# Shifting the pairs of chunks in the last batch of an attention and feed-forward kernel by one

## The chip, the cores and the metric

The kernel runs on one core of one Trainium2 chip. The metric is device time in microseconds (us); lower is better. A core has five engines that each run their own instructions in order: TensorE (PE; its weight loads are a row of their own, PEld), VectorE (DVE), ScalarE (ACT), GpSimd (POOL) and SyncE (SP). DMA transfers are issued from the queues of SP, ACT and POOL.

## The reference

```python
def _attn_ref(q, k, v, tau):                      # each (4, 5824, 256), f32
    qn = q / (norm(q, axis=1) + 1e-06)
    kn = k / (norm(k, axis=1) + 1e-06)
    s = kn.transpose(0, 2, 1) @ qn / tau          # (4, 256, 256)
    a = softmax(s, -1)
    return v @ a

def _moe_ref(x, w1, w2, w3, w_out):               # x = the attention's output, (23296, 256)
    return (((x @ w1) * (x @ w2)) @ w3) @ w_out   # w1, w2: (256, 1024), w3: (1024, 1024), w_out: (1024, 256)
```

For each of four batches, the small matrix of scores is folded into w1 and w2 (`Wf`), and w3 and w_out are multiplied into one matrix W (`W_sb`, 1024 x 256). What remains for a batch is: a = v Wf1, b = v Wf2, and the output (a * b) W.

## The kernel before, in words

**Chunks and blocks.** The 5824 tokens of a batch are cut into 12 chunks: 0 to 10 of 512 tokens and chunk 11 of 192. The 1024 columns of `Wf` are 8 blocks of 128. A *normal* block of a chunk (`normal`) is two matmuls for a and two for b, each of 512 columns; ACT casts a to bf16 (L988), DVE multiplies it with b out of PSUM (L1020), and the result is a part of `abh`, the chunk's a * b.

**Blocks by seven.** In the last batch (3) some blocks of two neighbouring chunks, c and c+1, are made together by a scheme of Strassen's kind: seven matmuls of 512 columns (X, T, X, Y, X, Z, X in `by_seven`) in place of eight, for three ACT copies (Y, t, as) and four DVE operations (Z, bs, and two products into `abh`, L1054 to L1085). It needs sums of the weights (`wsum`, made by DVE when the weights are folded) and sums of the tokens (`tsum`, four POOL operations of 512 columns for a pair, L682 to L688). `BY_SEVEN` says for each pair how many of its 8 blocks are made that way; the other blocks of the pair are normal. `plan` writes the order of the normal blocks (`todo`), and for each block by seven the place in that order from which it may start, moved by `W_SHIFT`; `TOKENS_AHEAD` says how many places before it the token sums are queued.

**Outputs.** When all 8 blocks of a chunk are done, `queue_out` appends its output to the list `outs`, which leaves in order of `out_key`: only its first line may go on. The output is made in one of three ways. *Plain products* (chunks in `PLAIN`): 32 matmuls of 256 columns, in two halves of four steps (`emit_half`, L1101), one PSUM bank each. *Seven products* (all others): a second scheme of that kind, seven products of 8 matmuls of 128 columns (prodA, prodB, prodC, L830). It needs four sums of parts of `abh`, in order, each of 1024 columns: POOL makes them (L790, L792), or, for chunks in `BY_DMA`, transfers do: two plain ones from SP's queue that copy two parts (L808, L809), and four from POOL's queue that add into memory (L800). *Singles*: chunk 11, and in the last batch chunk 10 as well, are put out one block at a time as each is done (`single`, `emit_out`, L1141), into banks that stay taken; chunk 10 uses the banks G and out2, which the scores leave free in the last batch. The outputs of the last `LAG_END` blocks of chunk 11 are held back to the very end (`ends`).

**What sets the order.** The instructions of all engines are written out by a planner in the Python of the kernel. `now` holds its reckoning of each engine's time by fixed costs (`work_on`), `free` the time at which each bank is free. `step` picks, for PE's next few matmuls, what can start first: the normal line, up to two blocks by seven, or the first line of `outs`, which is hurried or held by a credit that keeps about `HALF_BACK` steps in store. POOL's work waits in `pool_line`; `pool_due` takes the allowed one that is due first, by the number of steps until it is needed times `STEP`, or for token sums by `SLOT` and `T_EARLY`. `B1_BIAS` weighs two ways for one operation of a block by seven: DVE alone (`bs`, L1073), or ACT and POOL (L1070). An agenda starts the loads of v (POOL's queue), each behind a `gate` on POOL, and, if chunk 0 is paired, its token sums at `TSUM` within the batch before.

In the kernel before, the last batch is made as pairs (0,1), (2,3), (4,5), (6,7), (8,9) with 3, 5, 5, 5 and 4 blocks by seven, and chunk 10 alone.

Of the kernel before, what the change touches and what calls it, by code (L numbers as in the profile page):

```python
# [11 lines left out]
F32 = DT.float32  # L12
BF16 = DT.bfloat16

P = 128
PIECE = 8
LAG_END = 2
BIG_BUFS = 31
HALF_BACK = 12
LANDING = 4.0  # L20
W_SHIFT = 1
STEP = 1.9
SLOT = 1.8
T_EARLY = 0.0
N_BIAS = 0
O_BIAS = 0.05
B1_BIAS = -0.5
MM_COL = 1.0 / 2400.0
MM_FIX = 0.0025

# [2 lines left out]
def kernel(  # L33
# [14 lines left out]
    B, N, C = q.shape  # L48
    T, D = out.shape
# [15 lines left out]
    NCH = NT // 4 + 1  # L65
# [80 lines left out]
    turned_v, turned_at = {}, {}  # L146
# [404 lines left out]
        )  # L551


    BY_SEVEN = {(3, 0): 3, (3, 2): 5, (3, 4): 5, (3, 6): 5, (3, 8): 4}
    PAIRED = {b: tuple(c for b2, c in sorted(BY_SEVEN) if b2 == b) for b in range(B)}
    PLAIN = {0: (0, ), 1: (), 2: (), 3: (0, 2, 9, )}
    BY_DMA = {3: (4, 6, )}
    TSUM, WSUM0, TSUM0 = 100, 12.0, 26.0
    wsums = {}
    tsums = {}  # L560
# [95 lines left out]
    def queue_token_sums(b, c):  # L656

        until = now["PE"] + TOKENS_AHEAD * SLOT

        def step(i):  # L660
            def fn(at_):
                token_sum(b, c, i)
                if i == 3:
                    tready[b, c] = at_
            return fn

        for i in range(4):
            pool_add(
                lambda i=i: until - now["PE"] + 1.1 * (i - 3) - T_EARLY,
                (0.0, lambda: turned_at.get((b, c // 2), FAR) <= now["PE"], 1.06, step(i)),  # L670
            )

    tready = {}
# [81 lines left out]
    def out_bank(tag, ready=0.0):  # L755
        return max(free.get(tag, 0.0), ready)
# [133 lines left out]
    def plain_products(b, c, ab2, whole):  # L890

        for i in range(FT):
            yield lambda i=i: max(out_bank(f"out{i // 4}", whole), w_made[0])
            emit_half(b, c, i, ab2)

    def out_tags(b, c):
        return ("G", "out2") if (b, c) == (B - 1, NCH - 2) else ("out0", "out1")

    def single(b, c, j, ab, ready):

        yield lambda: max(
            ready, w_made[0], *(out_bank(t) for t in out_tags(b, c)), 0.0 if queued.get(b, 0) == NCH - 1 - b // (B - 1) else FAR
        )
        emit_out(b, c, j, ab)

# [40 lines left out]
    def finish(b, c, j, ready):  # L946

        key = b, c
        done_of.setdefault(key, []).append(ready)
        credit[0] = min(4.0, credit[0] + (1.0 if steps_left[0] > HALF_BACK else 0.8))  # L950
        if c == NCH - 1 or (b == B - 1 and c == NCH - 2):
            return
        if len(done_of[key]) == FT:
            queue_out(b, c, max(done_of[key]))
# [36 lines left out]
    def normal(b, c, j):  # L991

        n = chunk_cols(c)
        share_ = n / 512

        def both(w, t):
            for ct in range(CT):
                nc.tensor.matmul(  # L998
                    t[:, :n], lhsT=Wf[b][:, ct, w, j * P : (j + 1) * P], rhs=rhs_of(b, c, ct),
                    start=(ct == 0), stop=(ct == CT - 1),  # L1000
                )
            return work_on("PE", 2 * (n * MM_COL + MM_FIX))

        yield lambda: max(bank_at(), wready.get(b, 0.0))
        tag, t = take(f"a_{b}_{c}_{j}", cols=n)
        r = both(0, t)
        a_sb = cast(t, f"as_{b}_{c}_{j}", n)
        cast_at = free[tag] = work_on("ACT", 0.07 + 0.395 * share_, r)
        yield lambda: bank_at()
        tag, t = take(f"b_{b}_{c}_{j}", cols=n)  # L1010
        r = both(1, t)
        if c == NCH - 1:
            if b % 2 == 0 and j == 0:
                lefts[b // 2] = work.tile([P, FT, 2, P + LEFT], BF16, tag="left", name=f"left_{b}", bufs=1)
            two = lefts[b // 2][:, j, b % 2, :]
            nc.vector.tensor_mul(two, a_sb[:, :n], t[:, :n])
            ab = two[:, :P] if b % 2 == 0 else two[:, LEFT:]
        else:
            ab = place(b, c, j)
            nc.vector.tensor_mul(ab, two_halves(a_sb), two_halves(t))  # L1020
        ready = free[tag] = work_on("DVE", 0.065 + 0.533 * share_, r, cast_at)
        last_ab[:] = [ab, ready]
        finish(b, c, j, ready)
        if c == NCH - 1 and b == B - 1 and j >= FT - LAG_END:
            ends.append(lambda only=None: emit_out(b, c, j, ab, only))
        elif c == NCH - 1 or (b == B - 1 and c == NCH - 2):
            put_out(b, c, single(b, c, j, ab, ready), 1)

    ends = []
# [61 lines left out]
    def emit_half(b, c, i, ab2):  # L1091

        h, jj = divmod(i, 4)
        if i % 4 == 0:
            out_tiles[b, c, h] = psum.tile([P, 2, D], F32, tag=f"out{h}", name=f"o_{b}_{c}_{h}", bufs=1)
        if i == 0:
            out_tiles[b, c] = work.tile([P, 4, D], F32, tag="o_sb", name=f"osb_{b}_{c}", bufs=3)
        t, o = out_tiles[b, c, h], out_tiles[b, c]
        for j in (2 * jj, 2 * jj + 1):
            for k in range(2):  # L1100
                nc.tensor.matmul(  # L1101
                    t[:, k, :], lhsT=ab2[j // 4][:, h, j % 4, k * P : (k + 1) * P], rhs=W_sb[:, j, :],
                    start=(j == 0 and k == 0), stop=(j == FT - 1), skip_group_check=True,
                )
        work_on("PE", 4 * (D * MM_COL + MM_FIX))
        read = now["PE"] + LATE["PE"]
        if i == 3:
            nc.scalar.copy(o[:, 0:2, :], t)
            free["out0"] = work_on("ACT", 0.475, read)
        elif i == FT - 1:  # L1110
            if b == B - 1:
                nc.scalar.copy(o[:, 2:4, :], t)
                free["out1"] = work_on("ACT", 0.475, read)
            else:
                nc.vector.tensor_copy(o[:, 2:4, :], t)
                free["out1"] = work_on("DVE", 0.6, read)
            rows = out[b * N : b * N + NT * P, :].rearrange("(p i) c -> p i c", i=NT)
            nc.sync.dma_start(out=rows[:, 4 * c : 4 * c + 4, :], in_=o)

    def emit_out(b, c, j, ab, only=None):  # L1120
# [6 lines left out]
        else:  # L1127
            lhs = [ab[:, i // 2, i % 2 * P : (i % 2 + 1) * P] for i in range(4)]
        if j == 0:
            if b == B - 1 and not small:  # L1130
                held.update(("G", "out2"))
            out_tiles[b, c] = [
                psum.tile([P, 2, D], F32, tag=tag, name=f"o_{b}_{c}_{tag}", bufs=1)
                for tag in out_tags(b, c)[: len(lhs) if small else 2]
            ]
# [278 lines left out]
                c += 1  # L1414
        return todo, sevens

    TOKENS_AHEAD = 2
    token_at = {}
    stuck = [0]
    credit = [0.0]  # L1420
# [2 lines left out]
    def step(b, todo, sevens, at_n):  # L1423

        run_due()
        scores_due(progress[0])
        while later:
            later.pop(0)()
        pool_due()
        if lines["N"] is None and todo:  # L1430
            if (b, at_n[0]) in token_at and (b > 0 or at_n[0] > 0):
                queue_token_sums(b, token_at.pop((b, at_n[0])))
            lines["N"] = Line(normal(b, *todo.pop(0)))
            at_n[0] += 1
        while sevens and sevens[0][0] < at_n[0] and len(lines["W"]) < 2:
            lines["W"].append(Line(by_seven(b, *sevens.pop(0)[1:])))
        choices = [(max(now["PE"], w.est()), i, w) for i, w in enumerate(lines["W"])]
        if lines["N"] is not None:
            choices.append((max(now["PE"], lines["N"].est()) + N_BIAS, 3, lines["N"]))
        if outs:  # L1440
            hurry = credit[0] > 0.0 or steps_left[0] > 2 * HALF_BACK or not todo
            choices.append((max(now["PE"], outs[0].est()) + (-0.02 if hurry else O_BIAS), 4, outs[0]))
        if not choices:
            return
        when, kind, line = min(choices, key=lambda x: x[:2])
        if when > FAR / 2:
            now["PE"] += 0.2
            stuck[0] += 1
            assert stuck[0] < 1000, (b, at_n, choices, pool_line, held, progress, steps_left)
            pool_due()  # L1450
            return
        stuck[0] = 0
        more = line.go()
        if kind == 4:
            steps_left[0] -= 1
            line.left -= 1
            credit[0] = max(credit[0] - 1.0, -1.0)
            if not more:
                outs.pop(0)
        else:  # L1460
            progress[0] += 0.5 if kind == 3 else 2 / 7
            if not more:
                if kind == 3:
                    lines["N"] = None
                else:
                    lines["W"].remove(line)
# [55 lines left out]
```

## Time and profile before

| | us |
|---|---|
| median of 3 runs | 550.21 (550.02 to 550.28) |
| the profiled execution's own time | 550.1 |
| its span, from the first to the last instruction | 548.1 |
| busy: PE, PEld | 536.1, 350.5 |
| busy: DVE, ACT, POOL | 426.5, 397.4, 416.0 |
| POOL: adds of 128x1024 (L790 and L792), one | 2.13 |
| POOL: token sums of 128x512, one | 1.15 |
| DVE: product of 128x512 (L1020), one | 0.685 |
| ACT: cast of 128x512 (L988), one | 0.563 |

The rows of the profile name a line of the kernel, the engine, the operation, output<-inputs by the program's names, the shapes and the count. A matmul's duration in the rows is longer than the distance from one to the next, since matmuls are pipelined and their ends are modelled; the distances between starts say what PE really does. The last batch's matmuls start at about 428 us; the last matmul of all starts at 543.51.

### The profile page before, as it was taken

The page shows a single profiled execution, that of the slowest core. Times are in us where ns is not written, and L with a number is a line of the kernel's source. Part 1 is how long each engine was busy: PE and PEld are TensorE (multiplying, and loading weights), DVE is VectorE, ACT ScalarE, POOL GpSimd, SP SyncE. Part 2 cuts the span into 40 slices and gives each one's busy share as a digit, 9 for nine tenths or more (in the row PEclk, how much of TensorE's full clock was granted, in tenths as well). Part 3 has the DMA queues.
Part 4 walks back from the last instruction along what each step waited for, and adds up shares of the span by engine and source line. Part 5 has one row for each costly group of instructions (what it writes and reads, how often), then busy time and mean ns, then how long its engine had stood idle before and what let it go on. Part 6 is the DMA issues. An engine that isn't in the chain of part 4 may idle for free.

```text
span 548.1 us, 12254 instructions
## 1 busy us (share of the span) xinstructions
PE 536.1 (98%) x4599; PEld 350.5 (64%) x4607; DVE 426.5 (78%) x750; ACT 397.4 (73%) x826; POOL 416.0 (76%) x343
## 2 busy tenths in 40 slices
PE   7799999999999999999999999999999999999996
PEld 4564566666677666666658666666666656566676
DVE  5477748999876888888766788888878688999962
ACT  5446648889777788888676888888777677777762
POOL 4270794979999499998996498979999946978560
PEclk9999999999999999999999999999999999999999
DMA  9999987994876848875582867776651335656513
GB/s 213 212 205 208 215 162 156 225 189 101 130 165 145 190 87 186 171 160 125 118 170 90 163 137 148 150 147 125 155 117 72 85 87 115 156 110 174 142 53 136
DMA packets 76747, 80.75 MB, mean 147 GB/s; under 512 B 54416, under 2 KB 59024, under 8 KB 76688
## 3 DMA queue, kind: packets, MB, share of 16 engines
q0 software_dynamic: 16816, 41.03, 42.7%
q1 hardware_dynamic: 59504, 38.22, 25.1%
q8 instruction: 36, 0.59, 0.4%
q10 hardware_dynamic: 368, 0.72, 0.4%
q14 instruction: 23, 0.19, 0.1%
HBM read 78.91 MB, written 23.86 MB: 187 GB/s over the span
## 4 chain that ended last, share of the span: by engine, by line
PE 92%; DMA 5%; issue 1%; ACT 1%; DVE 1%; POOL 0%; DVEq 0%; POOLq 0%
PE a L998 25%; PE b L998 25%; PE prodA L830 13%; PE prodC L830 6%; PE G L216 6%; PE X L983 3%; PE prodB L830 3%; DMA k<-in_k_dram 3%; PE o L1101 3%; PE fold L449 2%; DMA q<-in_q_dram 2%; PE w L1290 1%; PE o_out L1141 1%; PE Y L983 1%; PE Z L983 1%; PE T L983 1%
## 5 line engine op out<-in xcount | busy, mean ns | idle before, releaser
L1020 DVE TENSOR_TENSOR abh<-as,b 128x512 bf16<-128x512 bf16 x308 | 210.3, 685 | 66.8 <-ACT as L988 44.3
L988 ACT CAST as<-a 128x512 bf16<-128x512 f32 (+1 forms) x340 | 191.0, 563 | 68.3 <-PE a L998 55.6
L998 PE MATMUL a<-vT,Wf 128*128 128x512 bf16 x616 | 183.2, 379 | 0.2
L998 PE MATMUL b<-vT,Wf 128*128 128x512 bf16 x616 | 183.2, 379 | 0.0
L998 PEld LDWEIGHTS <-Wf 128*128 128x128 bf16 x1360 | 122.2, 98 | 76.9 <-issue 0.7
L790 POOL TENSOR_TENSOR S<-abh,abh 128x1024 bf16<-128x1024 bf16 x37 | 78.9, 2132 | 51.1 <-DVE abh L1020 34.5
L830 PEld LDWEIGHTS <-S 128*128 128x128 bf16 x1216 | 80.1, 98 | 23.1
L230 DVE TENSOR_TENSOR acc<-acc,sq 128x512 f32<-128x512 f32 x132 | 91.6, 694 | 1.2 <-ACT sq L213 0.3
L792 POOL TENSOR_TENSOR S<-S,abh 128x1024 bf16<-128x1024 bf16 x37 | 78.8, 2128 | 2.7
L792 POOL TENSOR_TENSOR S<-abh,S 128x1024 bf16<-128x1024 bf16 x37 | 79.4, 2147 | 0.1
L792 POOL TENSOR_TENSOR S<-abh 128x1024 bf16<-128x1024 bf16 x37 | 78.9, 2132 | 0.1
L830 PEld LDWEIGHTS <-abh 128*128 128x128 bf16 x968 | 64.1, 98 | 20.4 <-issue 0.5
L843 ACT COPY osb<-prodA 128x256 f32<-128x256 f32 x113 | 42.2, 373 | 16.5 <-PE prodA L830 16.0
L216 PE MATMUL G<-k,q 128*128 128x256 bf16 x276 | 52.4, 273 | 0.0
L216 PEld LDWEIGHTS <-q 128*128 128x128 bf16 x276 | 27.0, 98 | 32.1
L830 PE MATMUL prodA<-comb_T,S 128*128 128x128 bf16 x608 | 46.3, 219 | 0.0
L213 ACT ACTIVATE sq<-q 128x512 f32<-128x512 bf16 x69 | 43.9, 636 | 0.0
L213 ACT ACTIVATE sq<-k 128x512 f32<-128x512 bf16 x69 | 43.4, 629 | 0.0
L850 DVE TENSOR_TENSOR osb<-osb,prodC 128x256 f32<-128x256 f32 x76 | 31.5, 414 | 4.4 <-ACT osb L843 3.5
L130 POOL DMA_DIRECT2D q<-in_q_dram x27 | 15.2, 563 | 11.7 <-DMA q<-in_q_dram 5.6
L830 PE MATMUL prodB<-W_sb,abh 128*128 128x128 bf16 x312 | 23.8, 219 | 0.0
L830 PE MATMUL prodA<-W_sb,abh 128*128 128x128 bf16 x312 | 23.8, 219 | 0.0
(175 smaller groups left out, 649.2 us busy)
## 6 DMA issues: line engine op xcount, KB each, us to landing
out_dram<-osb SPq DMA_DIRECT2D x44, 512.0 KB, 3.4
k<-in_k_dram POOLq DMA_DIRECT2D x19, 512.0 KB, 8.2
v<-in_v_dram POOLq DMA_DIRECT2D x19, 512.0 KB, 6.7
q<-in_q_dram POOLq DMA_DIRECT2D x18, 512.0 KB, 5.3
w<-in_moe_w_dram POOLq DMA_DIRECT2D x4, 512.0 KB, 16.7
k<-in_k_dram POOLq DMA_DIRECT2D x4, 320.0 KB, 7.3
v<-in_v_dram POOLq DMA_DIRECT2D x4, 320.0 KB, 4.3
S<-abh SPq DMA_DIRECT2D x4, 256.0 KB, 3.0
```

What stands on the lines that cost most here:

```text
L213: nc.scalar.activation(out=sqs[0][:, :, part, :], in_=src[:, o : o + 2, :], func=AF.Square)
L216: nc.tensor.matmul(G[:, ct, :], lhsT=qt[:, i, ct * P : (ct + 1) * P], rhs=kt[:, i, :], start=(pr == 0 and part == 0 and ct == 0), stop=(pr ...
L230: nc.vector.tensor_add(accs[n], accs[n], sqs[0][:, part - 2])
L790: nc.gpsimd.tensor_add(x, a21, a22)
L792: nc.gpsimd.tensor_sub(x, *{2: (sums[1], a11), 3: (a11, a21)}.get(i) or (a12, sums[2]))
L830: nc.tensor.matmul(st[nm][:, i, :], lhsT=a[:, j, i * P : (i + 1) * P], rhs=w[j], start=(first and j == 0 and i == 0), stop=(j == 3), skip_ ...
L843: nc.scalar.copy(quarter(r, d), st[nm])
L850: nc.vector.tensor_add(quarter(r, d), quarter(r, d), st[nm])
L983: nc.tensor.matmul(dst, lhsT=lhsT, rhs=rhs, start=start, stop=True, skip_group_check=True)
L988: nc.scalar.copy(a_sb[:, :n], t[:, :n])
L998: nc.tensor.matmul(t[:, :n], lhsT=Wf[b][:, ct, w, j * P : (j + 1) * P], rhs=rhs_of(b, c, ct), start=(ct == 0), stop=(ct == CT - 1),)
L1020: nc.vector.tensor_mul(ab, two_halves(a_sb), two_halves(t))
```

## The change

In the last batch, the pairs become (1,2), (3,4), (5,6), (7,8), (9,10) with 3, 5, 5, 4 and 5 blocks by seven, and chunk 0 is made alone, of normal blocks. Plain products make the outputs of chunks 1, 3, 9 and 10; chunk 10 no longer goes out block by block but by plain products in the banks G and out2, queued when all its blocks are done. The sums of chunk 5 are made by transfers, in place of those of chunks 4 and 6. Seven settings of the planner change with it.

```diff
-LAG_END = 2
+LAG_END = 4
-W_SHIFT = 1
-STEP = 1.9
-SLOT = 1.8
-T_EARLY = 0.0
+W_SHIFT = -1
+STEP = 1.6
+SLOT = 2.2
+T_EARLY = 1.0
-B1_BIAS = -0.5
+B1_BIAS = -1.0
...
-    BY_SEVEN = {(3, 0): 3, (3, 2): 5, (3, 4): 5, (3, 6): 5, (3, 8): 4}
+    BY_SEVEN = {(3, 1): 3, (3, 3): 5, (3, 5): 5, (3, 7): 4, (3, 9): 5}
-    PLAIN = {0: (0, ), 1: (), 2: (), 3: (0, 2, 9, )}
-    BY_DMA = {3: (4, 6, )}
+    PLAIN = {0: (0, ), 1: (), 2: (), 3: (1, 3, 9, 10, )}
+    BY_DMA = {3: (5, )}
...  # queue_token_sums: the piece of the pair's second chunk must be turned
-                (0.0, lambda: turned_at.get((b, c // 2), FAR) <= now["PE"], 1.06, step(i)),
+                (0.0, lambda: turned_at.get((b, (c + 1) // 2), FAR) <= now["PE"], 1.06, step(i)),
...  # plain_products
-            yield lambda i=i: max(out_bank(f"out{i // 4}", whole), w_made[0])
+            yield lambda i=i: max(out_bank(out_tags(b, c)[i // 4], whole), w_made[0])
...  # single
-            ready, w_made[0], *(out_bank(t) for t in out_tags(b, c)), 0.0 if queued.get(b, 0) == NCH - 1 - b // (B - 1) else FAR
+            ready, w_made[0], *(out_bank(t) for t in out_tags(b, c)), 0.0 if queued.get(b, 0) == NCH - 1 else FAR
...  # finish
-        if c == NCH - 1 or (b == B - 1 and c == NCH - 2):
+        if c == NCH - 1:
             return
...  # normal
-        elif c == NCH - 1 or (b == B - 1 and c == NCH - 2):
+        elif c == NCH - 1:
             put_out(b, c, single(b, c, j, ab, ready), 1)
...  # emit_half
         if i % 4 == 0:
-            out_tiles[b, c, h] = psum.tile([P, 2, D], F32, tag=f"out{h}", name=f"o_{b}_{c}_{h}", bufs=1)
+            if (b, c) == (B - 1, NCH - 2):
+                held.update(("G", "out2"))
+            out_tiles[b, c, h] = psum.tile([P, 2, D], F32, tag=out_tags(b, c)[h], name=f"o_{b}_{c}_{h}", bufs=1)
...  # emit_out
-            if b == B - 1 and not small:
-                held.update(("G", "out2"))
...
-    TOKENS_AHEAD = 2
+    TOKENS_AHEAD = 1
```

## The prediction

> **What bounds the kernel now.** I read the page first, then the busy time by stage, then the order of TensorE's own instructions, and last the rows of the engines that feed it. From the page:
>
> ```profile
> span 548.1 us, 12254 instructions
> PE 536.1 (98%) x4599; PEld 350.5 (64%) x4607; DVE 426.5 (78%) x750; ACT 397.4 (73%) x826; POOL 416.0 (76%) x343
> PE 92%; DMA 5%; issue 1%; ACT 1%; DVE 1%; POOL 0%; DVEq 0%; POOLq 0%
> ```
>
> and all long waits of PE (us in total, times, longest):
>
> ```profile
> PE sqq L277 <- DMA q<-in_q_dram: 4.8, 4, 1.7
> PE warm_I-94_95 L248 <- DVE ones_pp L94: 1.4, 1, 1.4
> ```
>
> PE is busy nearly always, the chain that ended last is PE for 92%, and the two waits lie at the start of the program. But a busy PE is only an occupied one, so I looked at starts. In the windows of the last batch (columns: stretch, length, then busy us and count of PE, PEld, DVE, ACT, POOL, clock, DMA share, GB/s):
>
> ```profile
> 428.00:440.00 12.00, 11.95 (x99) 7.24 (x98) 9.15 (x16) 8.46 (x18) 9.50 (x9) 1.00 0.39 91
> 440.00:450.00 10.00, 9.91 (x54) 5.07 (x52) 8.41 (x14) 7.38 (x15) 3.53 (x2) 1.00 0.43 116
> 490.00:510.00 20.00, 20.00 (x181) 12.62 (x180) 18.58 (x33) 15.14 (x33) 17.72 (x15) 1.00 0.62 167
> 521.90:531.50 9.60, 9.60 (x94) 6.30 (x92) 5.99 (x11) 5.97 (x12) 8.41 (x4) 1.00 0.14 56
> ```
>
> The clock is 1.00 throughout. DVE is next to full from 450 to 521 (18.58 of 20) and half empty after; POOL is half empty at the start. The timeline of PE (start, us, count) gives what one matmul really takes:
>
> ```profile
> 445.90 0.38 PE L983 MATMUL T<-tsum,wsum 128*128 128x512 bf16 x1
> 446.36 0.59 PE L998 MATMUL a<-vT,Wf 128*128 128x512 bf16 x2
> 446.79 0.38 PE L983 MATMUL X<-tsum,wsum 128*128 128x512 bf16 x1
> 541.87 1.91 PE L1141 MATMUL o_out<-W_sb,left 128*128 128x256 bf16 x16
> ```
>
> Two matmuls of 512 columns and the next: 446.79 - 446.36 = 0.43, so 0.216 each. Sixteen of 256 columns: (1.91 - 0.27) / 15 = 0.109. The same reading gives 0.0825 for 192 columns and 0.0557 for 128. With those pitches I went through all starts from 428 to the last at 543.51: only four gaps over 0.03 us are more than the pitch, 0.25 at 446.36 (446.36 - 445.90 - 0.216), 0.05 at 457.46, 0.08 at 479.11, 0.05 at 518.47. A fifth, 0.216 at 429.39, is exactly one matmul: the groups count 21 T for 22 blocks by seven, so a record is missing and nothing stood still. **So the last batch holds 0.43 us of standing PE in 115.8 us; the rest is work at full pace.** The Trainium skill ("Perfetto Trace Analysis", section "Identifying the Most-Contended Engine") warns off matmul occupancy and has headroom read from LDWEIGHTS busy, here 64%. By that rule a third of the batch would be open, an estimate of 0.36 x 115.8 = 42 us; the starts above leave 0.43, and the measurement decides.
>
> The one larger gap, in the chain in order of time:
>
> ```profile
> 444.24 0.68 DVE abh L1020
> 444.92 0.61 DVE bs L1073
> 445.62 0.70 DVE abh L1078
> 446.36 0.59 PE a L998 x2
> ```
>
> Three DVE operations in a row, and PE waits for the bank that the last one frees.
>
> **The change part by part.** *PE's work.* Blocks by seven: 3+5+5+5+4 = 22 before, 3+5+5+4+5 = 22 after, 7 matmuls of 512 each in place of 8. Chunks by plain products: 0, 2, 9 and, one block at a time, 10 before; 1, 3, 9, 10 after: four each, 32 matmuls of 256 each. Chunks by seven products: seven each, 56 matmuls of 128 each. Chunk 11 and its 16 outputs stay. PE's sum does not move by one matmul, so the change can only move the 0.43 us, and what follows the last matmul.
>
> *Sums by transfers.* One chunk in place of two: four adds on POOL come, four issues of adding transfers go, and two plain 256 KB transfers of SP's queue.
>
> ```profile
> L792 POOL TENSOR_TENSOR S<-abh 128x1024 bf16<-128x1024 bf16 x5 | 10.7, 2133 | 0.0
> L790 POOL TENSOR_TENSOR S<-abh,abh 128x1024 bf16<-128x1024 bf16 x5 | 10.6, 2126 | 16.4 <-DVE abh L1078 13.2 <-DVE abh L1085 3.2
> L682 POOL TENSOR_TENSOR tsum<-vT 128x512 bf16<-128x512 bf16 x4 | 5.0, 1242 | 0.0
> ```
>
> Four adds are 4 x 2.13 = 8.5 us; the eight issues of adding transfers at L800 took 1028, 887, 884 and 858 ns by kind, 0.91 in the mean, so four give 3.65 back. The token sums of the first pair (four of 1.15, 4.6 us) move from the end of batch 2 into batch 3. POOL in the batch: 75.3 + 8.5 + 4.6 - 3.65 = 84.8 of 115.8. It has the room: its adds sat 16.4 us waiting for blocks. Queued behind the new additions on POOL are the gates and loads of v. Before, the loads of 433.4, 451.1 and 468.1 were used by token sums at 455.9, 474.9 and 496.4, 22 us or more later; the shifted pairs need them half a pair sooner (some 10 us), so 2 to 8 us of delay on POOL cost nothing. SP loses 512 KB of transfers and its stores wait for less.
>
> *Does a POOL add slow DVE?* DVE's product L1020 took 684 ns from 438.7 to 446.3, with POOL empty, and 686 from 484.1 to 491, with it full. No cost. The Trainium skill ("Trainium Architecture — The Big Picture", section "What this means for kernel authors") says that DVE and GpSimd share a port pair under an exclusive lock; taken bluntly it would add 8.5 us to a nearly full DVE. The rows above show no such lock for these forms.
>
> *The start.* Chunk 0 runs as eight normal blocks (one DVE operation per block, not four per pair of blocks by seven), so the row of three DVE operations behind the 0.25 us gap moves off the place where the batch starts. It can come back in the next pair: I bound the batch's gaps between 0 and 1.0 (twice the four of before and a bit) and take 0.3: the three small ones (0.18) and half of the 0.25.
>
> *The end.* Now the last pair (9, 10) has five blocks by seven. From the time T at which pair (7, 8) is done, PE still has: 5x7x0.216 + 6x4x0.216 = 12.7; chunk 11, 32 x 0.0825 = 2.6; chunks 7 and 8, 112 x 0.0557 = 6.2; chunks 9 and 10, 64 x 0.109 = 7.0; chunk 11's outputs 1.75; and what is left of earlier chunks, 1.3 by the three products left at 521.9 in this trace (bounds 0 and 3.1). Sum 31.6, so T = 543.8 - 31.6 = 512.2 (510.4 to 513.5). Outputs leave in order, so chunks 9, 10 and 11 (8.7) stand behind chunk 8's last product (0.45): POOL's last sum must be there by 543.8 - 9.2 = 534.6. It starts chunk 7's and 8's eight adds at T: 512.2 + 17.0 = 529.2; before, it ended at 531.46 and its product began at 532.46. If all the last token sums fall behind T, 533.8. Cover 5.4 or 0.8 us. DVE after T: 20 operations by seven at 0.688, 6 normal at 0.684, 4 to 6 joins at 0.417: 20 us, at the 93% of the full stretch 21.5, so 533.7; the 8.7 us of outputs behind it set the limit at 535.1. Cover 1.4 us. Both just fit, and in time: I put the cost at nothing.
>
> *After the last matmul.* The copies, the two stores of ACT's queue and the closing take 548.1 - 543.8 = 4.3 us and are the same. LAG_END 4 only holds back four blocks' outputs in place of two. Chunk 10's store was issued at 542.50 and lands 3.0 later; now ACT copies both halves, and if its products end at 543.8 - 1.75 = 542.0, a copy of 0.59 makes that 542.9 and 545.9, still 1.0 us ahead of the last small store (issued at 544.66, 2.3 to land). Nothing, while that 1.0 holds.
>
> *The other settings.* STEP scales the due times of all four-add sequences alike, so the batches before keep their order; B1_BIAS chooses a path through POOL (L1070) that this trace doesn't hold once, and -1.0 chooses it less. Nothing.
>
> Sum: span 548.1 - 0.43 + 0.30 = 548.0; the profiled execution was 550.1, so 2.0 lie around the span, and the median 550.21 is 0.1 over it: **550.1 us**. What a measurement of this kernel can tell from no change is about 0.2%, 1.1 us.
>
> **The rivals.** *POOL ends last (slower).* If the last token sums and the transfers' four issues both fall behind T, POOL's last sum is at 512.2 + 17.0 + 4.6 + 3.65 = 537.5, 2.9 past 534.6, and PE stands by as much: up to 553.1, likeliest 552.1 with half the issues and some work saved for it. It decides from the point at which chunk 8's last sum ends after 534.6. For it: chunks 7 and 8 are now both on POOL, back to back. Against: 16.4 us of idle POOL before such sums.
>
> *DVE ends last (same or slower).* If the last pair starts late or DVE stays below 93%, its last product comes up to 1.3 after 535.1: 550.4 to 551.5.
>
> *All gaps go (faster, but not by what counts).* 550.21 - 0.43 = 549.8. To pass 549.1, another 0.7 would have to come out of the 4.3 us after PE, which the change doesn't touch.
>
> **How the numbers follow.** The forecast (549.8 to 550.6) 0.55; DVE last 0.15, half of it over the bound; POOL last 0.23, all over it; all gaps gone 0.05; 0.02 for what I don't see. Faster than 549.1: 0.03. Slower than 551.3: 0.23 + 0.07 + 0.01 = 0.31. Same: 0.66. The range, 549.6 to 552.4, takes in the floor with 0.2 of scatter and the larger part of POOL's case; some 0.15 lie above.
>
> **What would show it.** Right: PE busy from 428 on as before, gaps of at most 0.5 us, POOL's last 128x1024 add over before 534.6, and the same 4.3 us after the last matmul. Wrong: a gap of 1 us or more on PE between 530 and 543 ahead of a prodC released by POOL (the POOL rival) or of an L1101 matmul released by DVE (the DVE rival); or a last store that is chunk 10's.

## The result and the profile after

The changed kernel takes 551.48 us (median of 10 runs, 551.34 to 552.00) against 550.25 (550.02 to 550.51) for the kernel before in the same comparison: ratio 1.0024, 95% interval 1.0015 to 1.0032. It is 1.2 us slower, just past the 0.2% that the prediction set as its bound. The page after:

```profile
span 549.4 us, 12254 instructions
PE 537.2 (98%) x4596; PEld 350.3 (64%) x4607; DVE 425.7 (77%) x749; ACT 398.5 (73%) x827; POOL 420.7 (77%) x343
PE 89%; DMA 6%; POOL 2%; ACT 1%; issue 1%; DVE 1%; POOLq 0%; ACTq 0%; DVEq 0%
```

PE is still busy 98%, but the chain that ended last now runs through DMA for 6% in place of 5%, and through POOL for 2% in place of 0%. Where that happens stands in the windows of the last batch (stretch, length, then busy us and count of PE, PEld, DVE, ACT, POOL, clock, DMA share, GB/s):

```profile
428.00:440.00 12.00, 12.00 (x100) 7.25 (x99) 6.75 (x12) 8.16 (x17) 9.54 (x9) 1.00 0.46 105
440.00:450.00 10.00, 10.00 (x75) 5.72 (x73) 9.07 (x15) 7.53 (x16) 7.42 (x5) 1.00 0.35 101
500.00:510.00 10.00, 9.81 (x89) 6.00 (x89) 8.59 (x16) 6.53 (x16) 9.92 (x9) 1.00 0.50 104
510.00:520.00 10.00, 9.38 (x91) 5.81 (x88) 8.16 (x14) 6.69 (x16) 8.30 (x6) 1.00 0.38 108
520.00:530.00 10.00, 9.95 (x92) 6.35 (x92) 9.57 (x17) 8.02 (x17) 9.92 (x6) 1.00 0.13 54
```

The start of the batch is better than before (DVE 6.75 busy of the first 12 us in place of 9.15, PE busy throughout to 450); most of PE's idle time lies between 500 and 520. By the distances between starts, as in the prediction, PE stands 0.08 us at 441.06, 0.15 at 458.38, 0.03 at 477.98, 0.09 at 502.27, 0.30 at 503.22, 0.78 at 511.44 and 0.15 at 515.10: 1.58 us in all, against 0.43 before. (Gaps of exactly one matmul are left out here too: the page counts 4596 matmuls for 4607 weight loads.) The difference of 1.15, and 1.22 between the starts of the last matmuls (544.73 and 543.51), is the loss. The two largest gaps, in PE's timeline (503.22 - 502.70 and 511.44 - 510.23, less one and two matmuls of 0.216), and then the waits of weight loads and matmuls from 428 on (total, times, longest):

```profile
502.70 0.38 PE L983 MATMUL X<-tsum,wsum 128*128 128x512 bf16 x1
503.22 0.62 PE L830 MATMUL prodA<-comb_T,S 128*128 128x128 bf16 x8
```

```profile
509.78 0.61 PE L830 MATMUL prodA<-comb_N,S 128*128 128x128 bf16 x8
510.23 0.59 PE L998 MATMUL b<-vT,Wf 128*128 128x512 bf16 x2
511.44 0.62 PE L830 MATMUL prodC<-comb_N,abh 128*128 128x128 bf16 x8 [0.62 <-DMA abh<-abh]
```

```profile
PEld L983 <- DVE Z L1054: 1.3, 4, 0.5
PEld L830 <- POOL S L792: 1.2, 3, 0.6
PEld L830 <- DMA abh<-abh: 1.1, 1, 1.1
PE prodC L830 <- DMA abh<-abh: 0.6, 1, 0.6
```

prodC<-comb_N,abh is chunk 5's first C product. It reads S1 = a21 + a22, which the adding transfer abh<-abh makes in place. (A weight load's wait need not stop PE as long: this one waited 1.1 us, and PE stood 0.78; the gap in the starts is what counts.) The chain in order of time and POOL's timeline lead to the cause:

```profile
500.72 4.52 POOL S L792 x2
505.24 0.06 POOL S L800
505.30 0.17 issue
505.46 5.93 DMA abh<-abh
511.40 0.05 issue
```

```profile
500.09 0.92 POOL L800 DMA_DIRECT2D S<-abh  x1
500.72 2.44 POOL L792 TENSOR_TENSOR S<-abh 128x1024 bf16<-128x1024 bf16 x1
502.80 2.43 POOL L792 TENSOR_TENSOR S<-abh,S 128x1024 bf16<-128x1024 bf16 x1
504.87 1.23 POOL L800 DMA_DIRECT2D S<-S  x1
505.46 1.55 POOL L800 DMA_DIRECT2D abh<-abh  x1
506.02 2.17 POOL L682 TENSOR_TENSOR tsum<-vT,vT 128x512 bf16<-128x512 bf16 x1
```

The transfer was issued 0.59 after another and landed 5.93 later. The planner reckons 4.0 (`LANDING`), and PE's order is fixed when the program is written, so the product stands first, whatever else PE could do. Before, the two transfers of this kind landed after 3.35 and 4.29 and their products came 1.8 and 3.5 after the landing. For the first of them, in the kernel before: POOL's timeline, the landings of all its adding transfers (L800), and the product in PE's timeline (495.84 + 3.35 = 499.19, and the product at 500.95):

```profile
494.19 0.90 POOL L800 DMA_DIRECT2D S<-S  x1 [0.69 <-DMA S<-abh]
495.84 0.88 POOL L800 DMA_DIRECT2D abh<-abh  x1 [0.76 <-DVE bs L1073]
496.40 1.50 POOL L682 TENSOR_TENSOR tsum<-vT 128x512 bf16<-128x512 bf16 x1
```

```profile
DMA to landing us min/median/max: 3.2/3.3/4.3
```

```profile
500.95 0.44 PE L830 MATMUL prodC<-comb_N,abh 128*128 128x128 bf16 x5
```

In the changed kernel, the issue at 500.09 sits between two of chunk 6's adds, the second and the third: the third ends at 503.16, and PE's product that reads it starts at 503.22, after 0.30 of standing.

### The profile page after: what moved, and what is told of

Same layout as the page of the kernel before. It is cut to its first block, busy times and chain, and to the rows that moved or that the text cites. A ratio compares the mean times of both kernels' runs of the same rounds, so it can differ in the third digit from the quotient of the medians.

```text
span 549.4 us, 12254 instructions
## 1 busy us (share of the span) xinstructions
PE 537.2 (98%) x4596; PEld 350.3 (64%) x4607; DVE 425.7 (77%) x749; ACT 398.5 (73%) x827; POOL 420.7 (77%) x343
## 4 chain that ended last, share of the span: by engine, by line
PE 89%; DMA 6%; POOL 2%; ACT 1%; issue 1%; DVE 1%; POOLq 0%; ACTq 0%; DVEq 0%
PE a L998 24%; PE b L998 24%; PE prodA L830 12%; PE prodC L830 6%; PE G L216 5%; PE o L1103 3%; PE prodB L830 3%; PE X L983 3%; DMA k<-in_k_dram 3%; PE fold L449 2%; DMA q<-in_q_dram 2%; PE w L1290 1%; POOL S L792 1%; DMA abh<-abh 1%; PE o_out L1141 1%; PE Z L983 1%
## 5 line engine op out<-in xcount | busy, mean ns | idle before, releaser
L790 POOL TENSOR_TENSOR S<-abh,abh 128x1024 bf16<-128x1024 bf16 x38 | 80.9, 2130 | 51.1 <-DVE abh L1020 49.2
L792 POOL TENSOR_TENSOR S<-S,abh 128x1024 bf16<-128x1024 bf16 x38 | 80.8, 2127 | 2.8
L792 POOL TENSOR_TENSOR S<-abh,S 128x1024 bf16<-128x1024 bf16 x38 | 81.2, 2138 | 0.1
L792 POOL TENSOR_TENSOR S<-abh 128x1024 bf16<-128x1024 bf16 x38 | 81.2, 2137 | 0.1
L830 PEld LDWEIGHTS <-abh 128*128 128x128 bf16 x952 | 62.8, 98 | 20.9 <-DMA abh<-abh 1.1
```

What stands on the lines that cost most here:

```text
L790: nc.gpsimd.tensor_add(x, a21, a22)
L792: nc.gpsimd.tensor_sub(x, *{2: (sums[1], a11), 3: (a11, a21)}.get(i) or (a12, sums[2]))
L830: nc.tensor.matmul(st[nm][:, i, :], lhsT=a[:, j, i * P : (i + 1) * P], rhs=w[j], start=(first and j == 0 and i == 0), stop=(j == 3), skip_ ...
```

## The experiments

Four theories. **L** (late landing): the loss is the waits for chunk 5's adding transfers, and what their issues cost on POOL. **P**: POOL has too much to add between 500 and 530, with chunks 6, 7 and 8 on it. **N**: the shift itself puts the blocks by seven where nothing covers their chains. **S**: the seven settings cost many small gaps. Each kernel was timed beside the kernel before on the same chip; ratios are to that. "Standing" is the sum of PE's gaps from 428 on, made as above from one profiled execution of each kernel; it is good to about 0.1 us.

**One wait taken away.** Chunk 5's first C product reads another part of abh.

```diff
-        r2 = product("C", sums[1], t1, True)
+        r2 = product("C", a22 if by_dma else sums[1], t1, True)
```

> The changed kernel, with chunk 5's product C reading a part of abh in place of the sum S1 that the transfer abh<-abh makes: the transfer is still issued and lands, but PE has nothing to wait for (the output of chunk 5 leaves that sum out). Every engine's order is the same. Theory L (late landing: PE stood 0.78 us at 511.44 because the transfer issued at 505.46 took 5.93 us to land): the gap ahead of prodC<-comb_N,abh goes, all other gaps stay, 551.48 - 0.78 = 550.7 (550.5 to 550.9). Theory P (POOL is short of room in that stretch, and PE would wait at the next sum anyway): the 0.78 comes back within 10 us at another product, 551.3 to 551.6. Theory S (the new settings cost many small gaps all over the batch): 551.3 to 551.6, too.

Measured 1.0031 (1.0019 to 1.0042), standing 2.38. The 0.78 went, and 1.59 came at chunk 5's second C product:

```profile
516.78 0.62 PE L830 MATMUL prodC<-W_sb,abh 128*128 128x128 bf16 x8 [1.42 <-DMA abh<-S]
```

L's 550.5 to 550.9 was missed. P had said that the time would come back within 10 us at another product, and it did, 5.3 us further on, and longer than P gave (551.93 against 551.3 to 551.6). But what PE waits for is the next transfer, not an add of POOL. It was issued at 511.40, and landed 5.34 later, where the changed kernel's took 3.41. So I took both waits away.

```diff
-        r3 = product("C", sums[4], w22)
+        r3 = product("C", a22 if by_dma else sums[4], w22)
```

> The changed kernel, with both C products of chunk 5 reading a part of abh in place of the sums S1 and S4: all four adding transfers are still issued, in the same order, but PE waits for neither (chunk 5's output leaves these sums out). Taking S1's wait away alone let PE stand 1.59 us at S4 instead. Theory L: now nothing comes back, the gap of 0.78 is gone and the others stay: ratio to before 1.0010 (1.0004 to 1.0016), PE standing about 0.8 us in the batch. Theory P or N (something else is short there, and PE would stand at another place): 1.0020 or more.

Measured 1.0012 (1.0003 to 1.0021), standing 0.78: the gap is gone and nothing comes back. The transfers still land late here (5.92 and 4.77), and nobody waits.

**The transfers taken away.**

```diff
-                nc.gpsimd.dma_start(out=dst, in_=src, accum_op=ALU.add)
```

> The changed kernel without the four adding transfers of chunk 5 (its output leaves these additions out); the planner still reckons with them, so all other instructions keep their order. Besides the waits, their issues on POOL are gone (0.92 to 1.55 us each), which stood ahead of chunk 6's last two adds. Theory L: the 0.78 and the 0.30 at chunk 6's third sum go, PE stands about 0.5 us: ratio 1.0004 (0.9998 to 1.0010), and the adds take 2.13 us, not 2.44. Theory N: 1.0015 or more.

Measured 0.9999 (0.9990 to 1.0008), standing 0.47, as good as the 0.43 before the change. The 0.30 at 503 went as well; POOL's timeline there, and the weight loads' wait for POOL, 0.3 in place of 1.2:

```profile
499.97 2.12 POOL L792 TENSOR_TENSOR S<-abh 128x1024 bf16<-128x1024 bf16 x1
502.05 2.13 POOL L792 TENSOR_TENSOR S<-abh,S 128x1024 bf16<-128x1024 bf16 x1
```

```profile
PEld L829 <- POOL S L792: 0.3, 1, 0.3
```

Without the issue ahead of it, the third add starts 2.09 after the second in place of 2.71, so 0.62 earlier, and takes 2.12, not 2.44. The shift, the new settings, and POOL's adds for chunks 6, 7 and 8 are all still in this kernel, in which nobody makes chunk 5's sums, and together they cost nothing beyond the 0.4 us that the interval leaves open: N and S fall as causes of the loss, and L holds. POOL keeps a share that no kernel here takes apart. In the chain of the changed kernel chunk 6's adds stand right ahead of the issue at 505.46, so they made the transfer late as well; those adds without the transfers cost nothing, but the transfers without those adds were not tried.

**A second chunk by transfers.** `BY_DMA = {3: (5, 7, )}`

> The changed kernel with two chunks' sums by transfers again, 5 and 7 (the kernel before had 4 and 6): POOL has one chunk's adds for each pair, as before, and 8.5 - 3.65 = 4.9 us less to do between 500 and 530, where it was 93 to 99% busy in the changed kernel. Theory P (POOL is the engine that is short in 500 to 530, and PE's stands are the outputs' first line waiting for it): PE stands about 0.5 us in the batch, ratio to before 1.000 to 1.001. Theory L (each chunk by transfers costs a wait, as these land after 4.4 to 5.9 us and not 4.0): two such waits, ratio 1.003 to 1.005. Theory N (the shift puts the blocks by seven where nothing covers their chains, whoever makes the sums): 1.0015 to 1.003.

Measured 1.0051 (1.0039 to 1.0064), standing 3.30. The gaps to 515 are those of the changed kernel to 0.02, and chunk 7 adds its own: 1.18 at its first C product, with a landing of 6.4 us, and 0.34 at a POOL add. P wanted a gain; L's 1.003 to 1.005 was right but for 0.0001.

```profile
531.90 0.62 PE L830 MATMUL prodC<-comb_N,abh 128*128 128x128 bf16 x8 [1.01 <-DMA abh<-abh]
```

**POOL relieved by chunk 7.** `PLAIN = {..., 3: (1, 3, 7, 9, 10, )}`

> The changed kernel with chunk 7's output by plain products: no sums for it, 8.5 us less on POOL between 500 and 530, and 32 matmuls of 256 in place of 56 of 128 on PE, 3.49 - 3.12 = 0.37 us more work. Theory P: the gaps of 1.65 us in the batch fall to 0.6 or less, ratio 1.000 to 1.0015. Theory L: chunk 5's transfers stay, with their gap of 0.5 to 1.5, and 0.37 comes on top: ratio 1.003. Theory N: 1.0025 to 1.0035.

Measured 1.0027 (1.0016 to 1.0037), standing 1.62, and 0.37 more work. POOL falls from 9.92 to 4.21 of 10 in the stretch from 520, and the gaps at 503 and 511 are as they were (0.30 and 0.78), so that P falls for chunk 7's adds; N's 1.0025 to 1.0035 holds the time too, and it is the kernel without the transfers that speaks against N:

```profile
520.00:530.00 10.00, 10.00 (x69) 5.97 (x68) 8.90 (x15) 7.96 (x17) 4.21 (x3) 1.00 0.13 52
```

**No transfers at all, POOL does the sums.** `BY_DMA = {3: ()}`

> The changed kernel with no chunk's sums by transfers: chunk 5's four adds go to POOL as well (8.5 us more there, four issues of 0.9 to 1.55 us fewer). Theory L: both gaps that hang on the transfers go (0.78, and the 0.30 behind the add that an issue lengthened from 2.13 to 2.44), 550.3 to 550.7. Theory P: POOL's adds for chunks 5 to 8 in a row end later than PE needs them, 552 to 554. Theory S: 551.3 to 551.6.

Measured 1.0015 (1.0007 to 1.0024), standing 1.81 in the profiled execution, which was a shorter one (550.8). The median is 550.97: L's 550.3 to 550.7 was too low, P's 552 to 554 too high by more. The two gaps are gone, but POOL is at 9.84 of 10 from 500 and 9.92 after, and gaps of 0.07 to 0.35 come in nine places from 497 on. Only part of them is POOL's: three weight loads waited 0.9 us in all for its adds; most of the gaps stand at blocks by seven and normal blocks, and what caused those was not taken further. So chunk 5's sums don't come free on POOL either, but there they cost no more than by transfers (1.0015 against 1.0024, with intervals that overlap).

**The planner told the truth about landings.** First `LANDING = 6.0`, which also moves the issues on POOL:

> The changed kernel with LANDING 6.0 in place of 4.0: the planner reckons that a transfer of sums lands 6 us after its issue, and puts chunk 5's waiting products later in PE's order, and the issue of abh<-abh behind one token sum. Theory L: PE has other work ahead of prodC_5, its gap falls from 0.78 to under 0.2, 550.6 to 550.9; the 0.30 gap of 503.22 (a POOL add lengthened by an issue beside it) may stay. Theory P: as long as before or longer, 551.3 to 552. Theory S: 551.3 to 551.6.

Measured 1.0021 (1.0012 to 1.0030), standing 1.39: the gap at chunk 5's first C product is gone, but issues fell elsewhere between chunk 6's adds, whose last one then kept PE for 0.39, and gaps of 0.35 and 0.19 came behind. L's size was missed; by the time alone this kernel lies nearer to what P and S gave. Then only the landing, with the issues' due times left alone:

```diff
-                made[i] = at_ + LANDING
+                made[i] = at_ + 5.5
```

> The changed kernel with the planner reckoning 5.5 us in place of 4.0 from an adding transfer's issue to its landing, and the due times of the issues left alone: POOL's order stays the same, PE's differs in some ten places, with chunk 5's waiting products later. Theory L: the 0.78 gap falls under 0.2, the 0.30 stays: ratio 1.0010 (1.0005 to 1.0016). Theory N: PE has nothing else to do there and stands as long: 1.0020 to 1.0028.

Measured 1.0017 (1.0008 to 1.0026), standing 1.20. The 0.78 is gone, the 0.32 of 503 stays, and 0.25, 0.14 and 0.13 come at blocks by seven between 511 and 516. Both forecasts were missed, L's by a little. Of 0.78 half is recovered: what PE has in place of the product isn't all ready either, and that is the part of N that this kernel shows.

**Why the transfer lands late.** Chunk 6's output store of 512 KB is held back until chunk 5's.

```diff
+            if (b, c) == (3, 6):
+                held_stores.append(store)
+                return
```

> The changed kernel with chunk 6's 512 KB store of the output (issued at 507.14, beside the transfer abh<-abh that lands late) held back until chunk 5's. If the store beside it is what made that transfer slow, abh<-abh lands 4.0 to 4.4 us after its issue in place of 5.93, and the 0.78 gap goes; if the transfer queued just ahead of it or POOL's token sums behind it are, it still takes 5.5 to 6. The time says less: if PE runs ahead by 0.78, the fetch of 16 KB of instructions that fell on the transfer of S4 without S1's wait (5.34 us to land) falls on it again, and PE stands there up to 1.6 us: ratio 1.001 to 1.0035.

Measured 1.0026 (1.0016 to 1.0035), standing 1.85. From the issue (L800) to the landing: the transfer abh<-abh and then all four, first in the changed kernel, then in this one:

```profile
abh<-abh POOLq DMA_DIRECT2D x1, 256.0 KB, 5.9
DMA to landing us min/median/max: 3.3/3.5/5.9
```

```profile
abh<-abh POOLq DMA_DIRECT2D x1, 256.0 KB, 4.6
DMA to landing us min/median/max: 3.3/4.2/4.8
```

abh<-abh took 4.61 in place of 5.93 and PE's gap there is gone; 1.04 came at the second C product, whose transfer took 4.80. So 1.3 us of the lateness are the store's. The rest over the 3.3 of a transfer alone, another 1.3, goes with the transfer S<-S issued 0.59 ahead. No kernel moved that issue alone, but the traces at hand agree: in the kernel before, the second abh<-abh, 0.58 behind S<-S, with no store and no token sum beside it, took 4.29, and the first, 1.65 behind S<-S and with a token sum right behind it, took 3.35. So a token sum behind it does not make it late. The DMA queues from 505 to 512, in the changed kernel, show the two side by side:

```profile
q0 software_dynamic: 288, 0.52, 42.9%
q1 hardware_dynamic: 144, 0.52, 19.6%
```

In the packets of this trace, POOL's queue moved 48 in half a microsecond alone, and 21 to 27 beside 21 to 27 of the store. The Trainium skill ("DMA: Bandwidth & Descriptors", section "Queues, rings and completion order") says that an engine takes turns between its queues packet by packet. The equal counts fit that; the turns themselves are not seen, as the records don't name the engine.

**The parts apart.** The old pairs with one chunk by transfers, `BY_DMA = {3: (6, )}`:

> The kernel before with its old pairs and settings, but one chunk's sums by transfers in place of two (6; chunk 4's go to POOL, which then has the adds of both 4 and 5 and the token sums of a pair, 17.0 + 4.6 = 21.6 us in about 20). Theory P: PE comes to stand 0.5 to 2 us behind these adds, ratio 1.001 to 1.004. Theory L: one chunk less with a late landing, ratio 0.999 to 1.0005. Theory N: as before, 0.999 to 1.0005.

Measured 1.0035 (1.0021 to 1.0048), standing 2.33. Here P holds: with chunks 4 and 5 both on it POOL is at 9.84 and 9.92 of 10 from 490 to 510, and PE's longest gap, 0.70, is its:

```profile
505.28 0.62 PE L830 MATMUL prodC<-W_sb,S 128*128 128x128 bf16 x8 [0.54 <-POOL S L792]
```

The old pairs with the new settings:

> The kernel before with its old pairs and two chunks by transfers, and the seven new settings. Theories P, L and N all put the loss elsewhere, but the settings were chosen for other pairs: blocks by seven two places earlier and token sums one place ahead. Theory S (the settings alone cost it): 1.002 or more. The others: 0.9995 to 1.0015.

Measured 1.0045 (1.0033 to 1.0058), standing 2.52. All expected too little but S. Its gaps, up to 0.57, lie in some fourteen places from 444 to 520.

The new pairs with the old settings:

> The shifted pairs with the seven settings of the kernel before (LAG_END 2, W_SHIFT 1, STEP 1.9, SLOT 1.8, T_EARLY 0.0, B1_BIAS -0.5, TOKENS_AHEAD 2). Chunk 5's sums are still by transfers, and the two issues S<-S and abh<-abh again follow each other on POOL with token sums behind them. Theory S: the loss goes with the settings, 550.0 to 550.6. Theory L: the second of the two issues again takes over 5 us to land, and PE's gap there is 0 to 1.5 us by where the planner puts the product, 551 to 552.5.

Measured 1.0049 (1.0036 to 1.0063), standing 3.37; its transfer abh<-abh landed after 4.52, its gaps are 0.1 to 0.4 each in some fifteen places, most between 517 and 538, and none is at that product. S is wrong of the changed kernel and L says too little: pairs and settings go together, each with the other's costs 2.5 to 2.8 us, together 1.2.

Over all kernels the time follows PE's standing to about 0.5 us: 0.43 before, 0.47 at ratio 0.9999, 0.78 at 1.0012, 1.58 at 1.0024, 2.38 at 1.0031, 3.30 at 1.0051. Furthest off is the kernel in which POOL makes all the sums, with 1.81 at 1.0015.

## Why the prediction was right or wrong

**Right.** PE's work did not change; the whole loss is standing PE in the last batch. The 0.25 us gap went (0.26 in three small ones to 478 in its place). DVE did not end last: after 515.10 PE has no gap, and the last pair's five blocks by seven are covered. POOL's last add ended at 531.0, later than the 529.2 reckoned but ahead of the 534.6 given, and the 8.5 us of chunk 7's adds cost nothing (the kernel with chunk 7 plain). From the start of the last matmul to the end come 4.7 us, against 4.6 before, and the last store wasn't chunk 10's: that one landed 2.0 us ahead of the last, not 1.0 (the 3.0 from issue to landing was the median of four stores; its own took 2.6 before and after). 551.48 lies in the range of 549.6 to 552.4, and the slower side had 0.31. That is luck: the range went so far for POOL's sake, and the 0.31 was for POOL or DVE ending last, neither of which happened.

**Wrong.** 550.1 was the likeliest case, within 0.2% of no change, and it was 0.24% slower. The step that failed is "Sums by transfers": it priced chunk 5's transfers by what they do to POOL's total (3.65 us given back for the four issues that go; the four that stayed took 4.56) and never asked when they land, nor how far ahead of its product each landed in the trace of before. Those rows were there: 3.35 and 4.29 from issue to landing, 1.8 and 3.5 us to spare. In the changed kernel the transfers lost their cover twice: chunk 6's adds come first on POOL, so that the first adding transfer, whose two inputs had landed by 496.1, is issued at 500.09; and the second and third then go out together, beside a store. The bound for the batch's gaps (0 to 1.0, value 0.3) came from the four gaps of before and held no term for them; they measured 0.78 and 0.30, of a standing of 1.58 in all.

**The rivals.** POOL was the right engine in the wrong place: not chunk 8's last sum at the end, but chunk 6's third, behind an issue, and for 0.30 and not 2 us. No rival named a transfer that lands late, though the change says that it moves them.

## What to carry to other kernels

Here the order was written ahead, and PE, busy 98%, lost its time where the reckoning was wrong: most of all for a transfer, reckoned at 4.0 us and landed after 5.93. Before moving work onto or among them, list each one's issue, its landing and the start of its reader, and treat the spare time between as the thing being changed. Taking one wait away can show the next, so take them away one by one and then all. Where POOL issues a transfer between its own operations, count the operation behind it as late by a part of the issue (0.62 of 0.92 us here) and as longer (2.44 for 2.13).

## What the runs showed of the hardware

A transfer of 256 KB that adds within on-chip memory, issued from POOL, landed 3.3 us after its issue alone, 4.3 to 4.75 when issued 0.6 behind another (the kernel before, the one with the store held back, the old pairs with the new settings), and 5.9 with a 512 KB store beside it as well. A POOL add of 128x1024 took 2.40 to 2.44 us beside an issue, 2.13 otherwise.

The second C product's transfer landed after 3.41 in the changed kernel and after 5.34, 4.77 and 4.80 in three kernels with nearly the same order. In those a fetch of 16 KB of instructions (the queue marked "instruction") ran during its data, from 514.04, 513.91 and 513.11 for 0.95 to 1.45 us; in the changed kernel it came at 514.71, when the data had passed. In the first of the three (no wait for S1) all of the transfer's packets of data were done by 514.35 but eight of 2 KB, and the first of these began at 514.98, as the fetch ended. That they share one of the 16 DMA engines is inferred from this; the records don't name the engine.

```profile
q0 software_dynamic: 127, 0.23, 33.0%
q8 instruction: 1, 0.02, 1.5%
```

(Queues from 513 to 517 of that kernel.) In these three kernels PE ran ahead by about the 0.78 that it didn't wait, and the fetch came 0.67 to 1.60 earlier. What sets its time is not shown.
